# Plain values in rows of four tokens, spread by VectorE's 32x32 transposes, in an attention and FFN kernel

## The chip, the cores and the metric

The kernel runs on one core of a Trainium2 chip. The metric is the device time of one execution in microseconds (us), the median over runs. The program is one launch; inputs and output are float32 in HBM, and the kernel computes in bf16 with float32 accumulation.

## The reference, cut to what matters

```python
# q, k, v: (8 batches, 8 heads, 576 tokens, 64); w_in (512, 2048), w_out (2048, 512)
rel = pos[:, None] - pos[None, :]
plain   = (rel >= 0) & (rel < 32)                        # heads 0..3
dilated = (rel >= 0) & (rel < 128) & (rel % 4 == 0)      # heads 4..7
attn = softmax(where(mask, q @ k.T / 8, -1e9)) ; a = attn @ v
x = a.transpose(0, 2, 1, 3).reshape(4608, 512)
out = relu(x @ w_in) ** 2 @ w_out
```

Attention is local: a query of a plain head sees 32 tokens, one of a dilated head 32 tokens of its own residue modulo 4. The FFN behind it has most of the arithmetic.

## The kernel before, in words

Tokens are handled in FFN tiles: four of 256 tokens, then seven of 512. For each tile, `ffn_groups` gives a list of groups: first-layer groups (line 971: 128x128 weights, products into a PSUM tile `pf`, then ReLU on ScalarE at line 984 and the square on VectorE at line 987, into `h2T`), and second-layer groups (line 1027, from `h2T` and `w_out_sb`). A program written out by hand says what is done between the groups. The string `PROGRAM` is split at `|`; its first stretch runs before the first group, and one stretch after each group. The order in which the steps are recorded is the order of each engine's instructions, under a manual schedule; the tile framework adds a semaphore wait wherever it finds that an instruction touches memory that an earlier recorded one writes or reads.

Batch 0 is done in the head, by `first_step`. Heads go in pairs e = 0..3 (0 and 1 plain, 2 and 3 dilated); part 0 is tokens 0 to 255, part 1 the other 320. The letters are: `L` in front of a colon, a load; `T`, TensorE transposes of q and k (line 794); `C`, their copies out of PSUM (lines 801 to 812); `B`, the mask bias into a score tile (line 824); `S`, scores (line 846); `E`, exponential (line 854) and, for part 1, the mask product on VectorE (line 857); `P`, values times probabilities (line 884); `D`, row sums (line 900); `L` and `X` followed by digits, the reciprocal by logarithm and exponential on ScalarE (lines 907, 910); `M`, the product with it on VectorE into `xT` (line 917), the FFN's input. `s28x183`, `w` and `W` are products of zeros (line 764) that TensorE makes between. `u`, `m` and `g` are mask copies; `r`, `R` and `z` are the postponed ReLU and squares of the first two tiles of groups (ReLU of the second at line 990, on VectorE).

Values go into `vbd`: for a pair e and a block i of 64 tokens, a 128x128 tile with the pair's two heads on the diagonal and zeros beside them. It has two buffers, used by batch parity.

- Plain values of batch 0, part 0 (`plain`): four float32 loads from the SP queue (line 1066), 256 bytes for each token, then step `h`: two casting copies on VectorE (line 1140) into blocks 0 to 3.
- Plain values of batch 0, part 1: software loads from the POOL queue (line 197, codes `L0:v1s` and `L0:v1t`), straight into blocks 4 to 8 of `vbd` in bf16, 64 by 5 pieces of 128 bytes each. Batches 1 and 2 have their plain values loaded at the same line (`L1:v0dp`, `L1:v1dp`, `L2:vwp`).
- Dilated values: loaded into `vd`, and for part 1 spread by copies (line 247, steps `G`).
- Step `N` zeroes half of the dilated blocks (lines 1048 and 1049).

All of a stretch's loads and steps are recorded in its order, so the loads of the first stretch, which stand at its start, are recorded ahead of all of the head's steps. On the POOL queue the loads use eight semaphores in turn: the load number n waits, before it is issued, until the load number n - 8 has landed.

Of the kernel before, what the change touches and what calls it, by code (L numbers as in the profile page):

```python
# [12 lines left out]
RES = 4  # L13
# [22 lines left out]
def _masks(by_residue: bool = False) -> np.ndarray:  # L36

    j = np.arange(64)[:, None]
    c = np.arange(96)[None, :]
    tok = 4 * (c % 24) + c // 24
    near = ((tok - j >= 0) & (tok - j < WIN)).astype(np.float32)
    kr, km = j % RES, j // RES
    cc = np.arange(64)[None, :]
    rem = ((kr == cc // 16) & (cc % 16 - km >= 0)).astype(np.float32)
    c = np.arange(96)[None, :]  # L50
    far = ((c - j >= 0) & (c - j < WIN)).astype(np.float32)
    one = np.concatenate([near, rem, far], axis=1)
    p = np.arange(128)
# [6 lines left out]
    return np.concatenate([both, ident], axis=1).astype(ml_dtypes.bfloat16)  # L60
# [3 lines left out]
def kernel(  # L64
# [9 lines left out]
    nc = tc.nc  # L74
# [34 lines left out]
    h2_pool = ctx.enter_context(tc.tile_pool(name="h2", bufs=2))  # L109
# [11 lines left out]
    mk = const.tile([P, 256 + P], bf16, name="mk")  # L121
# [13 lines left out]
    xT = const.tile([P, KT, RING], bf16, name="xT")  # L135
    rb = [{nm: const.tile([(80, P, 80)[i], 2 * H * RES * D], bf16, name=f"{nm}b{i}") for nm in "qk"} for i in range(3)]
# [46 lines left out]

    def load_v(b: int, parts, which="pdr"):
# [6 lines left out]
        i0, i1 = 4 * p0, 4 if p1 == 1 else NB  # L191
        sides = [(hl, slice(64 * hl, 64 * hl + 64)) for hl in range(2)]
        for what in which:
            if what in "pst":
                for e in {"p": (0, 1), "s": (0,), "t": (1,)}[what]:
                    for hl, rows in sides:
                        nc.gpsimd.dma_start(  # L197
                            dst[rows, e, i0:i1, rows],
                            v[b, 2 * e + (hl ^ crossed(b, e)), 64 * i0 : 64 * i1, :].rearrange("(i p) d -> p i d", p=64),
                        )  # L200
            elif what == "d" and b == 1:
# [58 lines left out]

    def k_flat(e: int):

        return kbd[:, e, :, :].rearrange("p i c -> p (i c)")[:, 0:S]

    def trans_k(e: int):
# [12 lines left out]
        copy(k_flat(e).rearrange("p (m r) -> p m r", r=RES), x.rearrange("p r m -> p m r"))  # L278
# [95 lines left out]
    def quadrants(scs, pvs):  # L374
# [16 lines left out]
        for n, (b, e) in enumerate(pvs):  # L391
# [16 lines left out]
            for g, rows in enumerate(sides):  # L408
# [5 lines left out]
                def vrow(i):  # L414
                    return vbd[b % 2][rows, e, i, rows] if b == XB else v_rows[b % 2][rows, e, i, :]
# [108 lines left out]
    def batch1(code: str):  # L524
# [40 lines left out]
        elif what in "cp":  # L565
            nm, copy = code[1], nc.scalar.copy if code[3:] == "a" else nc.vector.tensor_copy
            x = two.pop((nm, int(what == "c")))
            if what == "c":
                copy(both_x[:, int(nm == "k"), H:, m0 : m0 + n], x)
            elif nm == "q":  # L570
                copy(qT[:, 0:2, :, m0 : m0 + n], x.rearrange("p (e r) m -> p e r m", r=RES))
            else:
                copy(
                    k_nat[:, :, RES * m0 : RES * m0 + w].rearrange("p e (m r) -> p e m r", r=RES),
                    x.rearrange("p (e r) m -> p e m r", r=RES),
                )
# [40 lines left out]
        elif what == "b":  # L617
# [6 lines left out]
            for e in (2, 3, 0, 1):  # L624
# [10 lines left out]
                for g, rows in enumerate(sides):  # L635
# [19 lines left out]
                    else:  # L655
                        y = 0
                        for i, _, q0, q1 in blocks(1, e, part):
                            z = RES * (q1 - q0)
                            to, rhs = slice(q0 - m0, q1 - m0), byr(two["n", e][rows, y : y + z])
                            P_.append((f"o{e}", o[cols, :, to], vbd[1][rows, e, i, rows], rhs, z))  # L660
# [107 lines left out]
    def first_step(code: str):  # L768
# [28 lines left out]
        elif what == "C":  # L797
# [9 lines left out]
            else:  # L807
                copy(qk0[:, 0, e, :, m0 : m0 + n], x[:, 0, :, :])
                nc.vector.tensor_copy(
                    xx[0][:, 1, S * e + RES * m0 : S * e + w + RES * m0].rearrange("p (m r) -> p m r", r=RES),  # L810
                    x[:, 1, :, :].rearrange("p r m -> p m r"),
                )
# [131 lines left out]
    def ffn_groups(tk0: int, nt: int):  # L944
# [4 lines left out]
        h2 = h2_pool.tile([P, NF, NT], bf16, name="h2T")  # L949
# [50 lines left out]
        def g1(i):  # L1000
# [5 lines left out]
            elif i < 4 and tk0 == 2 * NT:  # L1006
                for u, x in ((0, 0), (0, 1), (1, 0), (1, 1), (2, 0), (2, 1), (0, 2), (1, 2),
                             (2, 2), (3, 0), (3, 1), (3, 2), (0, 3), (1, 3), (2, 3), (3, 3))[4 * i : 4 * i + 4]:
                    mm1(u, kts[x : x + 1])
# [50 lines left out]
    plain = osb_pool.tile([P, DM], f32, name="osb")[:, :].rearrange("p (e i d) -> p e i d", e=2, d=D)  # L1060
# [3 lines left out]
    for e in range(2):  # L1064
        for hl, rows in enumerate(sides):
            nc.sync.dma_start(
                plain[rows, e, :, :], v[0, 2 * e + hl, 0:256, :].rearrange("(i p) d -> p i d", p=64)
            )
# [3 lines left out]
    near = mk[:, 0:96].rearrange("p (r m) -> p r m", r=RES)  # L1072

    def put(dst, src):
        nc.scalar.copy(dst, src)
# [4 lines left out]
    def masks(part):  # L1080
# [5 lines left out]
        if part:  # L1086
            put(r4(mask_p[:, 352:384]), near[:, :, 16:24])
            put(mask_p[:, 384:768].rearrange("p (i c) -> p i c", c=96), mk[:, 0:96].unsqueeze(1).broadcast_to([P, 4, 96]))
            put(r4(mask_p[:, 768:832]), near[:, :, 0:16])
            put(md[:, :, 0:32], mk[:, 224:256].unsqueeze(1).broadcast_to([P, RES, 32]))  # L1090
            put(md[:, :, 32:112], mk[:, 160:240].unsqueeze(1).broadcast_to([P, RES, 80]))
            put(mask_d[:, 704:768], mk[:, 96:160])
# [28 lines left out]
    def run(code):  # L1121
# [12 lines left out]
        elif code == "N":  # L1134
            zero_halves(vbd[0][:, NE // 2 :, 0:8, :])
        elif code[0] == "G":
            spread_v(0, int(code[1]), [int(code[2])], nc.scalar.copy if code[3:] else nc.vector.tensor_copy)
        elif code == "h":
            for rows in sides:
                nc.vector.tensor_copy(vbd[0][rows, 0:2, 0:4, rows], plain[rows, :, :, :])  # L1140
# [46 lines left out]
    for x, code in enumerate(("Q00", "Q01", "Q10", "Q11")):  # L1187
        steps.append((50 + x, 1, XB, code))
# [115 lines left out]
```

## Time and profile before

| | |
|---|---|
| time, median of 3 runs | 296.27 us (296.17 to 298.16) |
| the profiled execution: its time | 295.88 us |
| its span in the trace | 294.1 us |
| TensorE busy | 286.2 us, 97% |
| VectorE / ScalarE / GpSimd busy | 155.5 / 187.2 / 123.2 us |
| chain that ended last | TensorE 93% of the span |

A span is measured from the first to the last instruction of the trace; 1.8 us of the run lie around it. Times below are us from the start of the span. In a line of the timeline stand start, duration, engine, source line, operation, tile written and tiles read, shape, and count; the bracket at its end says how long the engine stood idle before it and what it waited for. A duration is that of the whole merged run of equal instructions; neighbours overlap by some hundredths of a us. PE is TensorE, DVE is VectorE, ACT is ScalarE, and POOL rows of DMA_DIRECT2D are the issues of software loads.

### The profile page before, as it was taken

The page shows a single profiled execution, that of the slowest core. Times are in us where ns is not written, and L with a number is a line of the kernel's source. Part 1 is how long each engine was busy: PE and PEld are TensorE (multiplying, and loading weights), DVE is VectorE, ACT ScalarE, POOL GpSimd, SP SyncE. Part 2 cuts the span into 40 slices and gives each one's busy share as a digit, 9 for nine tenths or more (in the row PEclk, how much of TensorE's full clock was granted, in tenths as well). Part 3 has the DMA queues.
Part 4 walks back from the last instruction along what each step waited for, and adds up shares of the span by engine and source line. Part 5 has one row for each costly group of instructions (what it writes and reads, how often), then busy time and mean ns, then how long its engine had stood idle before and what let it go on. Part 6 is the DMA issues. An engine that isn't in the chain of part 4 may idle for free.

```text
span 294.1 us, 7899 instructions
## 1 busy us (share of the span) xinstructions
PE 286.2 (97%) x3213; PEld 165.8 (56%) x3241; DVE 155.5 (53%) x452; ACT 187.2 (64%) x381; POOL 123.2 (42%) x208
## 2 busy tenths in 40 slices
PE   8999999999999999999999999999999999999994
PEld 6689647859555554555455545554554455445443
DVE  2785224647779566685659465947454245004300
ACT  6888545887667774988567656766676476127411
POOL 8686266847626965776763696000000000000000
PEclk9999999999999999999999999999999999999999
DMA  8999999999999999999999698012101210121022
GB/s 120 199 188 214 203 225 197 193 169 190 162 230 141 140 157 199 138 159 171 179 176 116 97 170 144 2 37 73 36 2 39 71 38 0 37 74 33 0 71 71
DMA packets 84211, 35.75 MB, mean 122 GB/s; under 512 B 53600, under 2 KB 79424, under 8 KB 84176
## 3 DMA queue, kind: packets, MB, share of 16 engines
q0 software_dynamic: 49056, 18.49, 56.5%
q1 hardware_dynamic: 34976, 16.67, 28.0%
q8 instruction: 25, 0.41, 0.6%
q10 hardware_dynamic: 144, 0.10, 0.1%
q14 instruction: 10, 0.08, 0.1%
HBM read 37.50 MB, written 9.44 MB: 160 GB/s over the span
## 4 chain that ended last, share of the span: by engine, by line
PE 93%; ACT 1%; issue 1%; DMA 1%; DVE 1%; POOL 0%; ACTq 0%; POOLq 0%
PE pf L1027 42%; PE pf L971 41%; PE po L369 2%; PE pa L369 2%; PE pf L369 1%; DMA kb<-in_k_dram 1%; ACT h2T L984 1%; PE pa L794 1%; PE pd L369 1%; PE pf L846 1%; DVE h2T L987 1%; PE po L764 1%; PE pa L564 0%; DVE qT L335 0%; PE po L884 0%
## 5 line engine op out<-in xcount | busy, mean ns | idle before, releaser
L971 PE MATMUL pf<-xT,w_in 128*128 128x512 bf16 (+1 forms) x697 | 127.6, 340 | 0.4
L1027 PE MATMUL pf<-w_out_sb,h2T 128*128 128x512 bf16 (+2 forms) x571 | 126.0, 373 | 1.6 <-issue 0.6
L984 ACT ACTIVATE h2T<-pf 128x512 bf16<-128x512 f32 x143 | 83.9, 600 | 32.3 <-PE pf L971 32.0
L971 PEld LDWEIGHTS <-w_in 128*128 128x128 bf16 x704 | 78.0, 113 | 46.3 <-issue 0.3
L987 DVE TENSOR_TENSOR h2T<-h2T 128x512 bf16<-128x512 bf16 x144 | 60.0, 424 | 61.5 <-ACT h2T L984 59.6
L1027 PEld LDWEIGHTS <-h2T 128*128 128x128 bf16 x592 | 56.1, 98 | 63.9
L321 POOL DMA_DIRECT2D vbd<-in_v_dram x80 | 43.5, 560 | 23.6 <-DMA kb<-in_k_dram 9.7
L1033 ACT COPY osb<-pf 128x512 f32<-128x512 f32 (+1 forms) x34 | 19.5, 574 | 50.5 <-PE pf L1027 50.5
L175 POOL DMA_DIRECT2D qb<-in_q_dram x19 | 13.7, 722 | 8.3 <-DMA xx<-qb 4.6
L713 ACT ACTIVATE rec<-rec 128x576 f32<-128x576 f32 x24 | 16.4, 683 | 0.7
L175 POOL DMA_DIRECT2D kb<-in_k_dram x19 | 13.3, 698 | 5.8 <-DMA w_in<-in_moe_w_in_dram 1.9
L197 POOL DMA_DIRECT2D vbd<-in_v_dram x16 | 11.0, 687 | 8.9 <-DMA kb<-in_k_dram 5.3
L730 ACT ACTIVATE pt<-pa 128x384 bf16<-128x384 f32 (+1 forms) x26 | 11.7, 498 | 4.5 <-DVE xT L720 3.8
L307 POOL DMA_DIRECT2D vd<-in_v_dram x20 | 12.0, 615 | 3.2 <-PE pa L369 2.1
L313 POOL DMA_DIRECT2D vbd<-in_v_dram x20 | 12.0, 618 | 3.2 <-PE pf L369 1.9
L716 DVE TENSOR_TENSOR xT<-pf,rec 128x512 bf16<-128x512 f32 x11 | 7.6, 692 | 10.5 <-ACT rec L713 10.5
L716 DVE TENSOR_TENSOR xT<-po,rec 128x512 bf16<-128x512 f32 x13 | 9.0, 691 | 6.5 <-ACT rec L713 6.3
L732 DVE TENSOR_TENSOR pt<-pt,mask_n 128x384 bf16<-128x384 bf16 (+1 forms) x20 | 7.2, 374 | 8.6 <-ACT pt L730 8.5
L732 DVE TENSOR_TENSOR pt<-pt,mask_f 128x384 bf16<-128x384 bf16 x24 | 8.4, 355 | 6.1 <-ACT pt L730 5.9
L369 PEld LDWEIGHTS <-vbd 64*64 64x64 bf16 x328 | 8.4, 107 | 4.4 <-issue 4.0
L337 DVE COPY qT<-xx 64x576 bf16<-64x576 bf16 (+1 forms) x30 | 10.5, 351 | 0.6
L730 ACT ACTIVATE pt<-pf 128x448 bf16<-128x448 f32 (+1 forms) x18 | 8.6, 519 | 1.0 <-PE pf L369 0.9
(156 smaller groups left out, 280.5 us busy)
## 6 DMA issues: line engine op xcount, KB each, us to landing
qb<-in_q_dram POOLq DMA_DIRECT2D x7, 320.0 KB, 6.8
kb<-in_k_dram POOLq DMA_DIRECT2D x7, 320.0 KB, 8.0
vd<-in_v_dram POOLq DMA_DIRECT2D x34, 64.0 KB, 4.5
w_out_sb<-in_moe_w_out_dram POOLq DMA_DIRECT2D x4, 512.0 KB, 13.0
out_dram<-osb SPq DMA_DIRECT2D x16, 128.0 KB, 5.0
qb<-in_q_dram POOLq DMA_DIRECT2D x6, 256.0 KB, 6.4
kb<-in_k_dram POOLq DMA_DIRECT2D x6, 256.0 KB, 8.8
out_dram<-osb SPq DMA_DIRECT2D x9, 160.0 KB, 3.7
```

The source lines that it names most:

```text
L175: nc.gpsimd.dma_start(t[p0 : p0 + n, part, h0:h1, :], src[b, h0:h1, t0 : t0 + RES * n, :].rearrange("h (p r) d -> p h (r d)", r=RES),)
L321: nc.gpsimd.dma_start(v_rows[b % 2][p0 + 16 * r : p0 + 16 * r + 16, e, :, :], v[b, 2 * e + hl, :, :].rearrange("(i m r) d -> r m i d", r=R ...
L369: nc.tensor.matmul(out, lhs, rhs, start=begin, stop=True, skip_group_check=True)
L713: nc.scalar.activation(rec[:, :], rec[:, :], ACT.Exp, scale=-1.0)
L716: nc.vector.tensor_tensor(out=tok[:, :, 16:M], in0=byr(o[:, :]), in1=byr(rec[:, 0:512]), op=ALU.mult)
L730: nc.scalar.activation(pt, sp[b, e][g][:, 0:n], ACT.Exp, scale=SCALE)
L732: nc.vector.tensor_tensor(out=pt, in0=pt, in1=mask, op=ALU.mult)
L971: nc.tensor.matmul(to, w_in_sb[piece][:, kt, c0 : c0 + 509 : 4], rhs, start=(kt == kts[0] and x == 0), stop=(kt == kts[-1] and x == per - ...
L984: nc.scalar.activation(hv, acc[u][:, :].rearrange("p (x n) -> p x n", x=per), ACT.Relu)
L987: nc.vector.tensor_tensor(out=hv, in0=hv, in1=hv, op=ALU.mult)
L1027: nc.tensor.matmul(cur[m][:, c0:c1], h2[:, f, P * m : P * m + P], w_out_sb[:, f, c0:c1], start=(f == 0), stop=(f == NF - 1),)
L1033: (nc.vector.tensor_copy if last and part == 1 or tk0 == 3 * NT // 2 else nc.scalar.copy)(osb[:, c0:c1], cur[m][:, c0:c1])
```

## The change

Plain values of batches 0 to 2 are loaded in rows of four tokens: partition 32f + x holds, for one head, the 256 values of the tokens 8x + 4f to 8x + 4f + 3 of a part. Such a load goes into the second halves of the `h2T` tiles, which the 256-token tiles do not use; `h2T` becomes two fixed tiles in place of a pool. A new step `A` (`place`) spreads a part: one VectorE 32x32 transpose over float32 words (two bf16 values each) within the staging tile, then further ones into `vbd`, two for batch 0 (one for each half of the partitions) and one for batches 1 and 2. The order of the tokens within a block that comes out is (f, m, r) for token 8m + 4f + r, so keys (`keys`) and masks are put into the same order: a key copy becomes two copies, and for part 1 or a whole sequence three.

The last 64 tokens (block 8) do not fit the pattern and get loads of their own, code `u`. The first part of batch 0 still comes from SP, as float32 in the new rows, with a casting copy `Z` into the staging tile. In the first stretch the steps `P00 P10 D00 D10 L00` move from behind `T31` to ahead of `S20`, three mask copies move from ScalarE to VectorE, `C31` from ScalarE to VectorE, `N` to the start, and most of the products of zeros go.

```diff
-    "L0:q001 L0:q023 L0:q123 L0:v0d L0:i0 L0:q101 L0:v1d L0:i1a L0:i1b L0:v1s L0:i2a L0:v1t L0:i2b L0:i3 L0:o0 L0:o1 "
-    "L0:o2 L0:o3 L1:q00123 y L1:q10123 L1:v0dp s28x183 T00 C00a T10 C10a B00 B10 w1 S00 E00 B20 W1 S10 E10 N u B30 W1 "
-    "w1 T20q w1 T20k C20v T30 C30v h W1 w1 S20 E20 w1 S30 E30 T21 C21v T31 C31a G20 G30 P00 P10 D00 D10 L00 X00 P20 "
-    "P30 D20 D30 L20 X20 M00 j S21 S31 w1+31 M20 E21 E31 G21 G31a | T01q T11q | T01k C01v T11k C11a r P21 P31 D21 D31 "
-    "R S01 S11 L21 X21 M21 L31 X31 M31 z E01 E11 | L2:q00123 L2:q10123 L1:v1dp |  | P01 D01 L01 X01 M01 P11 D11 L11 "
...
+    "L0:q001 L0:q023 L0:q123 L0:v0d L0:i0 L0:q101 L0:v1d L0:i1a L0:i1b L0:v1s L0:v1t L0:i2a L0:v1u L0:i2b L0:i3 L0:o0 "
+    "L0:o1 L0:o2 L0:o3 L1:q00123 y L1:q10123 L1:v0pd Z s40x128 T00 C00a T10 C10a B00 B10 S00 E00 B20 S10 E10 A00 u B30"
+    " T20q w1 T20k C20v T30 C30v P00 P10 D00 D10 L00 S20 E20 w1 S30 E30 T21 C21v T31 C31v X00 M00 P20 P30 D20 D30 L20 "
+    "X20 M20 G20 G30 S21 S31 w1+31 w1+31 j E21 E31 G21 G31a | T01q T11q | T01k C01v T11k C11a r P21 P31 D21 D31 R S01 "
+    "S11 L21 X21 M21 L31 X31 M31 A01 E01 E11 z | L2:q00123 L2:q10123 L1:v1pud |  | P01 D01 L01 X01 M01 P11 D11 L11 X11"
...
-    h2_pool = ctx.enter_context(tc.tile_pool(name="h2", bufs=2))
+    h2T = [const.tile([P, NF, NT], bf16, name=f"h2T{i}") for i in range(2)]
...
+    def fours(b: int, part: int):
+        x = 4 * (3 * (part == 0) if b == 0 else part + (b == 1))
+        t = h2T[b // XB]
+        return t[:, x : x + 2, NT // 2 :], t[:, x + 2 : x + 4, NT // 2 :]
+
+    def place(b: int, part: int):
+        x, y = (t.bitcast(f32) for t in fours(b, part))
+        nc.vector.transpose(y.rearrange("p e (x r) -> p e r x", r=RES), x.rearrange("p e (r x) -> p e r x", r=RES))
+        y = y.rearrange("p e (i x) -> p e i x", i=4)
+        at = slice(4 * part, 4 * part + 4)
+        for rows, cols in [(rows, rows) for rows in sides] if b == 0 else [(slice(0, P), slice(0, D))]:
+            nc.vector.transpose(vbd[b % 2][rows, 0 : NE // 2, at, cols].bitcast(f32), y[rows])
...
-                            dst[rows, e, i0:i1, rows],
-                            v[b, 2 * e + (hl ^ crossed(b, e)), 64 * i0 : 64 * i1, :].rearrange("(i p) d -> p i d", p=64),
+                            fours(b, part)[0][rows, e, :],
+                            v[b, 2 * e + (hl ^ crossed(b, e)), 256 * part : 256 * part + 256, :].rearrange("(x f r) d -> f x (r d)", f=2, r=RES),
...
+            elif what == "u":
+                for hl, rows in sides:
+                    nc.gpsimd.dma_start(
+                        dst[rows, 0 : NE // 2, NB - 1, rows if b == 0 else slice(0, D)],
+                        v[b, (slice(hl, H // 2 - hl, 3 - 2 * hl) if b else slice(hl, H // 2, 2)), 512:S, :].rearrange("h p d -> p h d"),
+                    )
...
+    def keys(copy, to, x, some: bool):
+        n = x.shape[2] - 16 * some
+        for f in range(2):
+            copy(
+                to[:, 0 : RES * n].rearrange("p (i f m r) -> p f i m r", f=2, m=8, r=RES)[:, f],
+                x[:, :, 0:n].rearrange("p r (i m f) -> p f i m r", m=8, f=2)[:, f],
+            )
+        if some:
+            copy(to[:, RES * n :].rearrange("p (m r) -> p m r", r=RES), x[:, :, n:].rearrange("p r m -> p m r"))
...
-        elif code == "h":
-            for rows in sides:
-                nc.vector.tensor_copy(vbd[0][rows, 0:2, 0:4, rows], plain[rows, :, :, :])
+        elif code == "Z":
+            nc.vector.tensor_copy(fours(0, 0)[0], plain[:, :].rearrange("p (e x) -> p e x", e=2))
+        elif code[0] == "A":
+            place(int(code[1]), int(code[2]))
```

The rest of the diff follows from this: later stretches of `PROGRAM` get `A10`, `A11`, `A20` and `A21` for batches 1 and 2, whose loads come as `L1:v0pd`, `L1:v1pud` and `L2:vwpu`; one q copy of batch 2 is made a group earlier, and two products of the fifth tile change places.

More of the change, by code (lines that the diff above doesn't have):

```diff
@@ L52, in _masks @@
     one = np.concatenate([near, rem, far], axis=1)
+    placed = near.reshape(8, 2, RES, 96).transpose(1, 0, 2, 3).reshape(64, 96)
     p = np.arange(128)
@@ L59, in _masks @@
         return np.concatenate([turned[:, 0:96]] * 4 + [close], axis=1).astype(ml_dtypes.bfloat16)
-    return np.concatenate([both, ident], axis=1).astype(ml_dtypes.bfloat16)
+    last = near.reshape(64, RES, 24)[:, :, 0:16].reshape(64, 64)
+    both = np.concatenate([np.concatenate([placed] * 2, axis=0), both[:, 96:], ident, np.concatenate([last] * 2, axis=0)], axis=1)
+    return both.astype(ml_dtypes.bfloat16)
 @with_exitstack
@@ L119 @@
     nc.scalar.preload_act_table_set("natural_log_exp_and_others")
-    mk = const.tile([P, 256 + P], bf16, name="mk")
+    mk = const.tile([P, 256 + P + 64], bf16, name="mk")
     ident = mk[:, 256 : 256 + P]
@@ L414, in vrow @@
                 def vrow(i):
[L415 removed]
+                    if b > XB:
+                        return v_rows[b % 2][rows, e, i, :]
+                    return vbd[b % 2][rows, e, i, rows if dil else slice(0, D)]
                 P_, D_ = [], []
@@ L572, in batch1 @@
             else:
[L573 to L576, printed above, removed]
+                for e in range(NE // 2):
+                    keys(copy, k_nat[:, e, RES * m0 : RES * m0 + w], x[:, RES * e : RES * e + RES, :], part)
         elif what == "s":
@@ L948, in ffn_groups @@
         early = NT <= tk0 <= 3 * NT
-        h2 = h2_pool.tile([P, NF, NT], bf16, name="h2T")
+        h2 = h2T[len(made) % 2]
+        made.append(tk0)
         per = NT // nt
@@ L1059 @@
             nc.scalar.copy(to, none)
-    plain = osb_pool.tile([P, DM], f32, name="osb")[:, :].rearrange("p (e i d) -> p e i d", e=2, d=D)
+    zero_halves(vbd[0][:, NE // 2 :, 0:8, :])
+    plain = osb_pool.tile([P, DM], f32, name="osb")
     nc.vector.tensor_scalar(
@@ L1063 @@
     )
-    for e in range(2):
-        for hl, rows in enumerate(sides):
+    for hl in range(2):
+        for f in range(2):
+            p0 = 64 * hl + 32 * f
             nc.sync.dma_start(
-                plain[rows, e, :, :], v[0, 2 * e + hl, 0:256, :].rearrange("(i p) d -> p i d", p=64)
+                plain[p0 : p0 + 32, :].rearrange("p (e x) -> p e x", e=2),
+                v[0, hl : H // 2 : 2, 0:256, :].rearrange("e (x f r) d -> f x e (r d)", f=2, r=RES)[f],
             )
```

27 lines of the change are left out of this document (11 added, 16 removed), and 12 rows, old and new, of the table PROGRAM.

## The prediction

> **What bounds the kernel now.** I read the page's first lines, then PE's waits, then PE's timeline, because the change works on the first 14 us alone and moves little behind them.
>
> ```profile
> span 294.1 us, 7899 instructions
> PE 286.2 (97%) x3213; PEld 165.8 (56%) x3241; DVE 155.5 (53%) x452; ACT 187.2 (64%) x381; POOL 123.2 (42%) x208
> ...
> PE po L764 <- DVE kbd L1051: 1.1, 1, 1.1
> ...
> PE pf L846 <- issue: 0.6, 1, 0.6
> PE pa L794 <- DMA kb<-in_k_dram: 0.3, 1, 0.3
> ```
>
> PE is the bound. The longest single waits of it are 1.1 us before the first instruction, 0.6 us in which nothing visible holds it, and 0.3 us for the first keys. All of them lie in the head. The timeline and the stretches show the rest:
>
> ```profile
> 9.06 0.29 PE L794 MATMUL pa<-mk,kb 64*64 64x64 bf16 x8
> ...
> 11.21 0.49 PE L884 MATMUL pf<-pt,vbd 128*128 128x96 bf16 x8
> 11.53 0.48 PE L900 MATMUL pf<-pt,ones 128*128 128x96 bf16 x8
> ...
> 14.38 1.04 PE L971 MATMUL pf<-xT,w_in 128*128 128x256 bf16 x8
> ...
> 18.84 2.81 PE L971 MATMUL pf<-xT,w_in 128*128 128x256 bf16 x24
> ...
> 1.07:4.42 3.35, 3.35 (x23) 3.30 (x24) 0.47 (x4) 3.31 (x4) 3.15 (x5) 1.00 0.71 117
> 4.42:4.98 0.56, 0.56 (x8) 0.42 (x5) 0.00 (x0) 0.53 (x2) 0.56 (x2) 1.00 1.42 205
> 5.00:14.38 9.38, 8.46 (x214) 5.77 (x214) 6.05 (x18) 6.78 (x18) 6.98 (x12) 1.00 1.33 188
> 14.38:18.84 4.46, 4.46 (x97) 3.76 (x96) 3.65 (x10) 3.39 (x9) 4.16 (x6) 1.00 1.41 194
> ```
>
> From the first FFN product (14.38) on PE is busy without a gap, so the time is the start of the FFN plus a fixed amount of PE work: what delays the head is not won back behind it, and what shortens the head is won in full. The head has 9.38 - 8.46 = 0.9 us of idle PE between 5.00 and 14.38.
>
> **The plain values: a new wait.** Before, the plain values of part 0 need SP's loads and two casting copies. The software loads of part 1 (L197) go to other blocks of the same tile, and the copies pass them:
>
> ```profile
> 9.81 0.86 DVE L1140 CAST vbd<-osb 64x512 bf16<-64x512 f32 x2
> ...
> 12.12 0.72 POOL L197 DMA_DIRECT2D vbd<-in_v_dram  x1
> 14.26 0.67 POOL L197 DMA_DIRECT2D vbd<-in_v_dram  x1 [1.42 <-DMA w_in<-in_moe_w_in_dram]
> ...
> 15.92 1.36 POOL L197 DMA_DIRECT2D vbd<-in_v_dram  x2
> 17.27 1.52 POOL L1105 DMA_DIRECT2D w_in<-in_moe_w_in_dram  x2
> ...
> L197 POOL DMA_DIRECT2D vbd<-in_v_dram x4: 674/686/722, 12.1 to 16.6; - x4
> ...
> DMA to landing us min/median/max: 4.7/5.1/5.3
> ```
>
> The copies run at 9.81, before any of those four loads is issued. In the changed program as built this is otherwise. The two transposes of A00 that write into `vbd` each wait for two DMA semaphores, at the value that the 21st and the 22nd software load bring them to. These are the two loads of `L0:v1u`, for the last 64 tokens. They stand ahead of A00 in the program, and write block 8 of the same tile; the transposes write blocks 0 to 3 through a float32 view of it. No byte is shared, but the wait is there. P00 on PE waits for the second of those transposes.
>
> So the question is when `u` lands. Load n is issued when load n - 8 has landed. Loads 16 to 22 were v1s, v1s, i2a, v1t, v1t, i2b, i3 (the POOL rows above, i2a's left out; the second of the last pair at about 18.0), and are v1s, v1s, v1t, v1t, i2a, u, u; what each waits for, loads 8 to 14, is unchanged. So `u` is issued at 17.3 and 18.0. The bytes queued ahead of it and with it are those of the old v1s, i2a and v1t, whose last was issued at 16.6 and landed 4.7 later, at 21.3. I take 21.3 for the second `u`: the queue was full then, and it holds as much now.
>
> ```profile
> L313 POOL DMA_DIRECT2D vbd<-in_v_dram x20: 586/611/657, 69.8 to 172.0; - x20
> ...
> DMA to landing us min/median/max: 2.3/4.5/7.4
> ```
>
> Line 313 issues loads of values into the same tile too. Bounds: its shortest landing gives 18.0 + 2.3 = 20.3, the longest of L197 18.0 + 5.3 = 23.3.
>
> The Trainium skill ("DMA: Bandwidth & Descriptors", section "Why a DMA increments its semaphore by 16 and not by 1") has a DMA run on the largest number of engines up to 16 that divides the slowest dimensions of both sides. The new four-token loads have 2 there, which would queue each on two engines and could bring `u` up to an estimated 1 us later; no run here shows it yet, and the upper bound holds it already.
>
> **What stands behind the wait.** VectorE works in order: behind A00 stand three mask copies (moved from ScalarE), C20, C30, C21, C31, M00. PE does its work up to T30 and stops at P00, which now stands ahead of S20. PE made T30's keys at 9.06 before, and with fewer zeros does so a little sooner. So it stands for about 12 us. Ahead of P00 the change thus gains nothing: the fewer zeros, `Z`, `A00`'s first transpose and the doubled part-0 key copies all end long before 21.3 and cost nothing under that cover.
>
> From 21.3 the chain is made of these rows:
>
> ```profile
> 9.14 0.76 DVE L801 COPY xx<-pa 128x512 bf16<-128x512 bf16 x2 [0.90 <-PE pa L794]
> 11.03 0.49 DVE L801 COPY xx<-pa 128x640 bf16<-128x640 bf16 x1 [0.36 <-PE pa L794]
> 11.44 0.21 DVE L803 COPY kbd<-pa 128x64 bf16<-128x64 bf16 x1
> 12.30 1.06 DVE L247 COPY vbd<-vd 64x256 bf16<-64x256 bf16 x4
> 13.39 0.69 DVE L917 TENSOR_TENSOR xT<-pf,rec 128x512 bf16<-128x512 f32 x1
> 14.00 0.46 DVE L1143 CAST vbd<-osb 64x128 bf16<-64x128 f32 x2
> ...
> 15.10 0.79 DVE L857 TENSOR_TENSOR pt<-pt,mask_d 128x512 bf16<-128x512 bf16 x2
> ...
> 17.13 0.33 DVE L808 COPY xx<-pa 128x320 bf16<-128x320 bf16 x1 [0.49 <-PE pa L794]
> 17.37 0.88 DVE L809 COPY xx<-pa 128x320 bf16<-128x320 bf16 x2
> 18.17 0.68 DVE L990 TENSOR_SCALAR h2T<-pf 128x512 bf16<-128x512 f32 x1
> ...
> 8.96 0.80 ACT L1075 COPY mask_d<-mk 128x128 bf16<-128x128 bf16 x3
> ...
> 12.05 0.60 ACT L907 ACTIVATE rec<-pf 128x512 f32<-128x512 f32 x1
> 12.68 0.63 ACT L910 ACTIVATE rec<-rec 128x512 f32<-128x512 f32 x1
> ```
>
> - The second spread transpose, 64 partitions by 512 bf16: no row has a transpose. Nearest is a copy of that size (0.86 / 2 = 0.43, from float32; a bf16 copy of half the size takes 0.26). I take 0.35; bounds 0.2 to 0.7. It ends at 21.65.
> - Mask copies: 0.80 for three on ScalarE; on VectorE I take 0.2 each, as the smallest copies there (0.21): 22.25.
> - C20, C30: 0.76, to 23.0. Meanwhile PE does P00, P10, D00, D10 (0.49 + 0.48 by the rows), then S20, S30 and T21, T31, to about 23.9.
> - C21 and now C31 as well on VectorE, 2 x (0.49 + 0.21) = 1.4, to 25.0; before, ScalarE took C31's large half.
> - M00 0.69, to 25.7. L00 and X00 (0.60 + 0.63 behind D00) are done by then. The first FFN product comes at 25.7 instead of 14.38: **+11.3**.
> - Then VectorE sets the pace up to the third FFN stretch: M20 behind X20, to 26.6 (I allow 0.2 of waiting); G20, G30 1.06; j 0.46; mask products of E21, E31 0.79; G21's two copies 0.5: 29.4. Then the key and query copies C01, C11 (0.33 + 0.88, and 0.3 more because each key copy is now three): 30.9; the postponed ReLU 0.68: 31.6. PE alone would be there at 25.7 + 4.46 = 30.2. Before, the third stretch began at 18.84, as that ReLU ended (18.17 + 0.68). So **+12.75**: the part of VectorE's head work that used to run during the head's PE work now stands behind the stall.
>
> Behind it A01 (three transposes, 1.1 by the value above) comes ahead of P01 and E01's mask product; PE has its 2.8 us of FFN meanwhile, and v1s and v1t have landed by 21.3, so I cost it at nothing. Without that cover it is at most its 1.1.
>
> **PE's clock.** PE's 183-column products show a cold start: 3.35 us hold 23 (146 ns each), the next 0.56 us hold 8 (70 ns each). A stop of 12 us may bring the slow state back. P00 to T31 hold about 1.8 us of PE work and the stretch behind some 4.5, of which VectorE hides much; I take +0.5, bounds 0 and 1.2.
>
> The Trainium skill ("TensorE: Matmul & The Clock Gate", section "Part 1: The HAM clock gate (the "warmup" mystery)") has the clock fall after some 3.4 us of idle and need as long of busy time to return. By it the upper half of those bounds would hold; the cold start agrees (146 against 70 ns), while no stop long enough to test the fall is in the trace.
>
> **The sum.** 294.1 + 12.75 + 0.5 = 307.35 us of span. The profiled execution took 295.88, 1.78 more than its span, so 309.1; the median (296.27) lies 0.4 above that execution: **309.5 us**. Bounds: landing -1.0 and +2.0, transpose -0.15 and +0.35, clock -0.5 and +0.7, VectorE's pieces about 0.7 either way. Added up in full they give 307.2 to 313.2, the likeliest case's own range.
>
> **Rival 1: no stall, not slower.** The place is A00, the deciding point whether `u` is in by about 9.5, when P00 could begin. Then P00, D00 and L00 run ahead of S20 and M00 comes earlier. The head's idle PE time bounds the gain: 1.1 us, which stays (it lies before the first instruction), and 0.9 us. I give it 0 to 0.6: 295.7 to 296.3. Against it: POOL issues the 22nd load at 18.0, and nothing ahead of it is taken out; the chip would have to pass a wait that stands in the program. A gain of over 1% (3 us) exceeds all idle time of the head, so it hardly exists.
>
> **Rival 2: the change doesn't do what it says.** The plain products come first, but the first FFN tile also needs M20, and X20 ahead of it now stands behind four more products of about 1 us (0.49 + 0.48 for the rows of two pairs). If M20 is what the first tile really waits for, the new order brings nothing even without a stall, and the time is the old 296.3. For it: the reciprocals run one behind the other on ScalarE, 0.60 + 0.63 us each by the rows above. With the stall it is a detail inside the 12.75.
>
> **Rival 3: a second stall.** A10 waits in the same way for `L1:v1u`.
>
> ```profile
> 43.88 0.70 DVE L616 TENSOR_TENSOR pt<-pt,mask_p 128x352 bf16<-128x352 bf16 x2
> ...
> 46.67 0.76 POOL L197 DMA_DIRECT2D vbd<-in_v_dram  x1
> 48.00 0.67 POOL L197 DMA_DIRECT2D vbd<-in_v_dram  x1 [0.58 <-DMA kb<-in_k_dram]
> ...
> DMA to landing us min/median/max: 4.4/6.6/10.0
> ```
>
> A10 stands behind that mask product, at 44.6, and with the shift at about 57.8. By its place in the queue `L1:v1u` has the slots of 46.67 and 48.00; the landings of 36 to 60 us (last row) put it at 52.4 to 58.0. So it is in by then, but narrowly. If the loads slip 1 to 3 us, PE loses up to 3 us again: 310.5 to 312.5.
>
> **How the numbers follow.** Forecast (one stall, 307.2 to 313.2) 0.84; second stall 0.08, within the same range; no stall or nothing done (rivals 1 and 2) 0.06; over 1% faster 0.02. About 1%, 3 us, is what a measurement of this kernel can tell from no change. Slower is the first two cases, 0.92; of the third 0.05 are the same and 0.01 a gain larger than I can name, which with the last makes faster 0.03. The range reaches down to 304.5, for a `u` that lands sooner than its bound and VectorE work that the stall hides after all, and up to 313.5.
>
> **What would show it.** Right: VectorE idle from about 9 to 21 before a transpose into `vbd`, ended by a DMA of values; PE idle about 12 us before line 884's first product; first FFN product at 24.5 to 28; third stretch 12 to 14 us later than 18.84; from there on the old timeline, shifted. The clock: the products behind the stall at double their old time for the first few us. Rival 3: a second idle of VectorE of that kind near 58. Wrong: no idle on VectorE over 2 us in the head, or `u` landing before 15; then the time is near 296 and the reading of the wait was mistaken. If the stall is there and the time is below 304, the PE work behind it was not fixed.

## The result: slower by 6.0%, more than forecast, and the profile after

The changed kernel takes 314.62 us (median of 6 runs, 312.22 to 315.76) against 296.26 us before: 1.0603 times, 95% interval 1.0557 to 1.0648. That is 18.4 us more; 13.2 were forecast, and the time lies 1.1 us above the range. The stall that was forecast is there, at its place and nearly with its length. What was mis-sized is the work behind it: PE's at a lower clock, VectorE's, and that of the later steps `A`. Every ratio here counts only runs within 1.5% of the fastest of their kernel, while a median counts all; of u_behind_zeros below it counts 303.01 and 305.29 us.

The first lines of the page of after (the slices of PEclk are 7.8 us each, 9 is full speed):

```profile
span 313.3 us, 7979 instructions
PE 291.0 (93%) x3220; PEld 169.0 (54%) x3248; DVE 162.9 (52%) x485; ACT 185.8 (59%) x379; POOL 129.1 (41%) x218
PEclk9555999999999999999999999999999999999999
```

Its waits, of VectorE:

```profile
DVE vbd L203 <- DMA vbd<-in_v_dram: 13.3, 1, 13.3
```

and of PE (total, times, longest):

```profile
PE pf L921 <- DVE vbd L203: 12.3, 1, 12.3
PE po L804 <- DVE kbd L1089: 1.1, 1, 1.1
PE pa L409 <- DVE kbd L388: 0.9, 1, 0.9
PE po L921 <- DVE pt L894: 0.6, 1, 0.6
```

VectorE stood 13.3 us at A00's transposes into `vbd` until a load of values landed, and PE 12.3 us behind it. PE's busy time also rose, by 4.8 us, although it does less: some of it ran at half speed. VectorE's timeline of after, with the two rows of A00 and the first copy of C21:

```profile
7.87 0.63 DVE L199 STREAM_TRANSPOSE h2T<-h2T 128x256 f32<-128x256 f32 x1
21.84 0.91 DVE L203 STREAM_TRANSPOSE vbd<-h2T 64x256 f32<-64x256 f32 x2 [13.35 <-DMA vbd<-in_v_dram]
...
26.12 0.49 DVE L841 COPY xx<-pa 128x640 bf16<-128x640 bf16 x1 [2.03 <-PE pa L834]
```

And PE's, from T30's keys to the fifth FFN stretch:

```profile
10.11 0.40 PE L834 MATMUL pa<-mk,kb 64*64 64x64 bf16 x8
22.81 0.77 PE L921 MATMUL pf<-pt,vbd 128*128 128x96 bf16 x8 [12.30 <-DVE vbd L203]
23.39 0.78 PE L937 MATMUL pf<-pt,ones 128*128 128x96 bf16 x8
...
29.69 1.92 PE L1009 MATMUL pf<-xT,w_in 128*128 128x256 bf16 x8
...
35.36 2.89 PE L1009 MATMUL pf<-xT,w_in 128*128 128x256 bf16 x24
38.88 0.39 PE L921 MATMUL po<-pt,vbd 128*128 128x32 bf16 x6 [0.64 <-DVE pt L894]
...
39.78 9.77 PE L1009 MATMUL pf<-xT,w_in 128*128 128x256 bf16 x88
```

The first FFN product came at 29.69 (before 14.38), the third stretch at 35.36 (before 18.84). The products behind the stall take 0.77 and 0.78 us where they took 0.49 and 0.48, and the first eight FFN products 1.92 where they took 1.04. The stretches of the timeline say why. After the colon stand the length, then busy time of PE, PEld, DVE, ACT and POOL, and behind them PE's granted clock, the DMA share and GB/s:

```profile
5.00:8.00 3.00, 1.93 (x50) 1.28 (x47) 1.36 (x6) 0.65 (x3) 3.00 (x6) 1.00 1.38 189
8.00:10.50 2.50, 2.50 (x43) 1.46 (x42) 0.49 (x1) 1.70 (x5) 1.65 (x4) 0.55 1.38 193
10.50:22.80 12.30, 0.01 (x2) 0.00 (x0) 0.89 (x3) 0.00 (x0) 9.74 (x16) 0.50 1.22 161
22.80:32.10 9.30, 9.29 (x145) 6.64 (x145) 5.93 (x18) 4.78 (x10) 4.91 (x7) 0.50 1.08 196
32.10:35.40 3.30, 3.30 (x79) 2.75 (x76) 2.85 (x12) 1.65 (x4) 0.73 (x1) 0.99 1.07 216
```

The granted clock was 0.50 through the stall and for 9.3 us of unbroken PE work behind it.

### The profile page after: what moved, and what is told of

Its sections match the earlier page's. It is cut to its first block, busy times and chain, and to the rows that moved or that the text cites. A ratio compares the mean times of both kernels' runs of the same rounds, so it can differ in the third digit from the quotient of the medians.

```text
span 313.3 us, 7979 instructions
## 1 busy us (share of the span) xinstructions
PE 291.0 (93%) x3220; PEld 169.0 (54%) x3248; DVE 162.9 (52%) x485; ACT 185.8 (59%) x379; POOL 129.1 (41%) x218
## 4 chain that ended last, share of the span: by engine, by line
PE 79%; DMA 11%; DVE 5%; POOL 2%; issue 1%; ACT 1%; SPq 0%; DVEq 0%; ACTq 0%; POOLq 0%
PE pf L1065 35%; PE pf L1009 35%; DMA xx<-qb 7%; DMA w_in<-in_moe_w_in_dram 2%; DVE h2T L1025 2%; PE po L409 2%; DMA vbd<-in_v_dram 1%; PE pa L409 1%; PE pf L409 1%; PE pa L834 1%; PE pd L409 1%; POOL qb L179 1%; POOL h2T L217 1%; PE pf L883 1%; POOL kb L179 1%
## 5 line engine op out<-in xcount | busy, mean ns | idle before, releaser
L361 POOL DMA_DIRECT2D vbd<-in_v_dram x80 | 43.6, 560 | 27.2 <-DMA kb<-in_k_dram 12.5
L217 POOL DMA_DIRECT2D h2T<-in_v_dram x20 | 13.3, 671 | 10.0 <-DMA w_out_sb<-in_moe_w_out_dram 3.6
L353 POOL DMA_DIRECT2D vbd<-in_v_dram x20 | 11.9, 613 | 5.1 <-PE pf L409 2.1
L921 PE MATMUL pf<-pt,vbd 128*128 128x96 bf16 (+3 forms) x17 | 1.2, 226 | 12.3 <-DVE vbd L203 12.3
```

Source lines behind the costliest of these rows:

```text
L217: nc.gpsimd.dma_start(fours(b, part)[0][rows, e, :], v[b, 2 * e + (hl ^ crossed(b, e)), 256 * part : 256 * part + 256, :].rearrange("(x f ...
L361: nc.gpsimd.dma_start(v_rows[b % 2][p0 + 16 * r : p0 + 16 * r + 16, e, :, :], v[b, 2 * e + hl, :, :].rearrange("(i m r) d -> r m i d", r=R ...
```

## The experiments

Each kernel is compared with the kernel before on its own chip. "Shift" below is how much later ScalarE's ReLU of the same FFN group ran than in the profile of before; a time given with a shift is the group's time there.

### Is the wait for `u` the stall, and is there nothing else?

**u_behind_both**: the loads `u` recorded behind the steps that waited for them.

```diff
- ... L0:v1t L0:i2a L0:v1u L0:i2b ... L1:v0pd Z ... E10 A00 u B30
+ ... L0:v1t L0:i2a Z ... E10 A00 L0:v1u L0:i2b ... L1:v0pd u B30
- L2:q10123 L1:v1pud | ... | 1s1 A11 |
+ L2:q10123 L1:v1pd | ... | 1s1 A11 L1:v1u |
```

> The changed kernel with the loads of the last 64 tokens recorded behind the transposes that were made to wait for them: in the first stretch L0:v1u and the loads that follow it stand behind A00 (the order on the POOL queue stays), and L1:v1u stands behind A11. Theory (the wait for u is the whole stall, and the rest of the loss is PE's half clock, which fell at about 8.3 us, ahead of the stall): the 12.3 us of idle PE go, the first FFN product comes at 15 to 18, but PE still runs part of the head at a granted clock of 0.5; time 297 to 301. Rival 1 (the clock fell only because of the stall, and the change is otherwise what it promises): 295 to 296.5. Rival 2 (the stall is the wait for the values themselves or for another load, not for u): 312 to 316 again.

Measured: 308.62 us, 1.0349 times before (1.0282 to 1.0416). The early stall is gone, and the clock still fell; but the time fits no expectation: it lies between the theory's and rival 2's. The shift was 4.1 us at 26 us and 13.2 from 89 us on. Where the other 9 came from stands in that kernel's waits of PE, in VectorE's timeline and in the stretches:

```profile
PE pf L1055 <- DVE h2T L189: 3.9, 1, 3.9
```

VectorE's timeline, A11 and the second transpose of A20:

```profile
59.50 0.66 DVE L189 STREAM_TRANSPOSE h2T<-h2T 128x256 f32<-128x256 f32 x1 [2.07 <-DMA h2T<-in_v_dram]
...
86.50 0.45 DVE L193 STREAM_TRANSPOSE vbd<-h2T 128x256 f32<-128x256 f32 x1 [4.96 <-DMA vbd<-in_v_dram]
```

The stretches of low clock (columns as above):

```profile
8.00:18.90 10.90, 10.90 (x187) 7.62 (x183) 6.49 (x21) 6.22 (x15) 7.69 (x13) 0.53 1.31 184
...
90.00:96.50 6.50, 5.92 (x79) 2.99 (x80) 2.86 (x8) 2.68 (x6) 4.66 (x9) 0.50 1.27 203
```

A11 (at 59.50) waits 2.07 us for its values and A20 (at 86.50) 4.96 us for the loads `u` of batch 2. PE, starved for 3.9 us by the latter, then runs 6.5 us at a clock of 0.50. In the changed kernel these steps began 11 and 12 us later (A11 at 70.46; A20's first transpose at 92.48, here at 80.91) and did not wait: the early stall had covered later ones.

**u_behind_A00**: the first stretch altered in the same way, `L1:v1pud` left in its place.

> As the one before, but only the first stretch is altered: L1:v1u stays ahead of A10. Theory: with the head no longer late, A10 is due near 46 to 49 us and waits for L1:v1u, which landed at 56.4 in the changed kernel and would land at 52 to 57; VectorE stands for 4 to 9 us and PE, fed by it, loses 2 to 8 us: time 300 to 307, and above the kernel without either wait. Rival (PE has enough work in hand, or the load is in by then): the same as the kernel without either wait, within 1 us.

Measured: 309.04 us, 1.0376 (1.0317 to 1.0436). The second stall of the prediction's rival 3 appeared, at its place, once the first one was out of the way. VectorE's timeline, PE's waits, and the stretches around it:

```profile
58.03 0.45 DVE L193 STREAM_TRANSPOSE vbd<-h2T 128x256 f32<-128x256 f32 x1 [7.09 <-DMA vbd<-in_v_dram]
```

PE's wait for it:

```profile
PE po L399 <- DVE vbd L193: 6.0, 1, 6.0
```

The stretches:

```profile
52.60:54.90 2.30, 0.00 (x0) 0.00 (x0) 0.00 (x0) 1.26 (x3) 0.48 (x1) 0.97 1.41 203
54.90:58.50 3.60, 0.00 (x0) 0.00 (x0) 0.47 (x2) 0.00 (x0) 2.93 (x6) 0.50 1.00 114
58.50:61.70 3.20, 3.17 (x39) 1.53 (x40) 2.82 (x11) 1.29 (x3) 3.20 (x6) 0.52 0.97 102
```

A10 waited 7.09 us, PE 6.0. Yet the total is that of the kernel without this wait (expected: above it, and 300 to 307). The delay of 6 us at A10 spared A11 and A20 theirs (none of VectorE's waits for a load belongs to them): one stall took the place of the others.

**pairs_apart**: the order of the changed kernel, with the writes to `vbd` cut by pairs.

```diff
-            nc.vector.transpose(vbd[b % 2][rows, 0 : NE // 2, at, cols].bitcast(f32), y[rows])
+            for e in range(NE // 2):
+                nc.vector.transpose(vbd[b % 2][rows, e, at, cols].bitcast(f32), y[rows, e])
-                        dst[rows, 0 : NE // 2, NB - 1, rows if b == 0 else slice(0, D)],
+                        dst[rows, e, NB - 1, rows if b == 0 else slice(0, D)],
```

> The changed kernel in its own order, but each transpose into vbd and each load u is cut in two, one for each pair e (two more transposes per step of batch 0, one more for the others; four loads u for a batch instead of two). Theory (the wait is no need of the data: a write to both pairs at once spans, from its first to its last address, the other's block 8, and cut by pairs the spans lie apart): no step A waits for a load u, the stall of 12.3 us goes as it did with u behind the steps, the clock still falls near 8 us; 304 to 310. Rival (the wait has another ground, such as the float32 view itself): 312 to 317.

Measured: 304.15 us, 1.0227 (1.0167 to 1.0287), in the expected range: no step A stalls for `u` (A10 and A11 wait 1.08 and 2.32 us for their values). The clock fell only at 13.94 in its profile, not near 8 us as expected, and came back at 17.35. A00's transposes in VectorE's timeline:

```profile
8.10 1.01 DVE L204 STREAM_TRANSPOSE vbd<-h2T 64x128 f32<-64x128 f32 x4
```

P00 and P10 in PE's:

```profile
9.23 0.49 PE L923 MATMUL pf<-pt,vbd 128*128 128x96 bf16 x8
```

So the wait was no need of the data, and no matter of the float32 view alone: it went when the stretches of memory from first to last address lay apart. That such stretches overlap is not enough for a wait either. In the kernel before, step `h` writes blocks 0 to 3 of both pairs at once, as bf16, and the loads `L0:v1s`, recorded ahead of it, write blocks 4 to 8 of pair 0, between its first and its last address; yet `h` ran at 9.81, before the first of them was issued at 12.12. Which of the differences makes the wait (the float32 view of the write, the load across both pairs) is not shown: this run cut the write and the load together. With the wait for `u` gone in either way the loss falls from 6.0% to 2.3 to 3.5%. The stall costs 7.5 to 11 us net (the difference of the ratios times 296 us), less than its 12.3.

### What did the zeros do?

**u_behind_zeros**: the kernel of u_behind_both with the zeros of before (`s28x183`, and `w1`, `W1` as in the old string up to P00).

> The kernel without either wait, and the products of zeros in the first stretch as they were before the change (28 of 183 columns at the start, then nine of 256 or 512 columns up to P00 instead of one). Theory (the clock falls near 8 us because the head's PE work has gaps since the zeros went): the granted clock stays at 1.00 through the head; time 295.5 to 297.5, and 1 to 4 us below the kernel with few zeros. Rival (the zeros only take PE time): 0.5 to 1.5 us above the kernel with few zeros, their own column time.

Measured: 306.69 us in the median (303.01 to 308.51), 1.0212 (1.0114 to 1.0309). The clock was 1.00 through the head, and ScalarE's first ReLU came 0.5 us later than before instead of 3.3. The total missed its range for the reason found above: between 54 and 69 us the shift grew from 3.3 to 9.6, and there stand a clock of 0.50 from 63.65 to 70.48 us of the run's own time and, ahead of it, A11's wait, in VectorE's timeline:

```profile
59.80 0.64 DVE L189 STREAM_TRANSPOSE h2T<-h2T 128x256 f32<-128x256 f32 x1 [3.34 <-DMA h2T<-in_v_dram]
```

**before_few_zeros**: the kernel before, with the few zeros.

```diff
- ... s28x183 T00 C00a T10 C10a B00 B10 w1 S00 E00 B20 W1 S10 E10 N u B30 W1 w1 T20q ... h W1 w1 S20 ...
+ ... s40x128 T00 C00a T10 C10a B00 B10 S00 E00 B20 S10 E10 N u B30 T20q ... h S20 ...
```

> The kernel before, with only the products of zeros of the first stretch thinned out as in the changed kernel (40 of 128 columns at the start instead of 28 of 183; one of 512 columns up to S20 instead of nine). Theory (without them PE has gaps in the head, the granted clock falls to 0.5 near 8 us and stays there until full-size products have run for some 3 us): first FFN product at 15.5 to 18 instead of 14.4, time 2 to 5 us above before. Rival (the zeros only take PE's time): 0 to 1 us below before, clock 1.00 throughout.

Measured: 296.54 us, 0.9983 (0.9942 to 1.0024): no difference. The clock did fall, but only from 11.09 to 14.50 us, and the first FFN product came at 15.20, 0.8 us later than before. The theory was right that it falls, and wrong on when it comes back (ahead of the first FFN product) and on its price, and the fewer zeros are no part of the 18 us by themselves.

### What is the half clock worth behind the stall?

**stall_filled**: zeros for the stall.

```diff
- ... T30 C30v P00 P10 ...
+ ... T30 C30v w45 P00 P10 ...
```

> The changed kernel with 45 products of zeros (512 columns each) on PE between T30 and P00, so that PE works while VectorE waits for u; nothing else differs, and the wait for u is kept. Theory (of the 18.4 us lost, 12.3 are the stall and 4 are the half clock behind it): the clock is back at 1.00 when P00 starts at about 22 to 23, the first FFN product comes at 25.5 to 27.5 instead of 29.7, the third stretch at 31.5 to 33.5 instead of 35.4; time 310 to 312.5. Rival (VectorE's chain sets the pace behind the stall, the slow products hide under it): the third stretch stays at 34.5 to 35.5 and the time at 313.5 to 315.

Measured: 316.94 us, 1.0642 (1.0570 to 1.0713): no gain, the theory's time is refuted. But P00 and the first FFN product, in PE's timeline, came where it says, and the third stretch (34.13) between its range and the rival's:

```profile
11.12 11.46 PE L794 MATMUL po<-kbd 128*128 128x512 bf16 x45
22.99 0.49 PE L911 MATMUL pf<-pt,vbd 128*128 128x96 bf16 x8 [0.41 <-DVE vbd L193]
...
27.27 1.04 PE L999 MATMUL pf<-xT,w_in 128*128 128x256 bf16 x8
...
34.13 2.86 PE L999 MATMUL pf<-xT,w_in 128*128 128x256 bf16 x24
...
94.87 0.23 PE L399 MATMUL pa<-qT,kbd 64*64 64x96 bf16 x2 [1.92 <-issue]
```

The first FFN product came 2.4 us sooner, the third stretch only 1.2: PE stood 1.56 us at 31.68 for a mask product that VectorE had behind step `j`, whose two casts took 1.98 us there and 0.48 in the changed kernel. Behind that PE lost the rest again, in waits like the 1.92 us of the last row for which the profile shows no cause but its own sequencer. To measure the clock alone, the later steps A had to go.

**after_again**, the changed kernel on the chip of the next three:

> The changed kernel once more, on the chip of the three runs beside it, so that they can be compared with it: 313 to 317, PE idle for 12 us ahead of P00, granted clock 0.50 from about 8 to about 32 us.

Measured: 314.05 us, 1.0611 (1.0556 to 1.0666). Here the clock fell only at 13.19 us, in the stall itself, and came back at 30.26: what it was before the stall did not change the time.

**stall_b0**: early stall and few zeros as in the change, batches 1 and 2 loaded as before, without A10 to A21.

```diff
- ... L1:v0pd ... L1:v1pud ... A10 ... A11 ... L2:vwpu ... A20 | | A21 ...
+ ... L1:v0dp ... L1:v1dp ... L2:vwp ...
```

> The changed kernel with its early stall and its few zeros, but with the plain values of batches 1 and 2 loaded as before and without A10, A11, A20, A21 (keys and masks keep the new order, so the output of these two batches is not the reference's). Theory (the 1.8 us that the changed kernel loses between 54 and 117 us come from those steps and their loads): the shift against before stays near 17.3 us from 40 us to the end; time 1 to 2.5 us below the changed kernel. Rival (they come from the split key copies or from DMA traffic that all versions have): the shift grows to 19 all the same.

Measured: 314.54 us, 1.0605 (1.0576 to 1.0634), not below the changed kernel. In its profile the `u` loads were issued 1.5 us later, and P00 ran at 23.91 instead of 22.86; why is not shown. Counted from there, the theory holds: the shift was 18.17 us at 26 us and 18.50 at the end, a growth of 0.3; in the two profiles of the changed kernel it grew by 1.8 and 1.6.

**stall_b0_filled**: the same with `w45`.

> As the one before, with 45 products of zeros between T30 and P00. It measures the price of the half clock behind the stall where no later wait covers it. Theory (12.55 us from P00 to the third FFN stretch with the half clock, 11.14 without it, since VectorE is the next bound): 1 to 2 us below the kernel without the filling, third stretch near 34. Rival 1 (PE's whole slow stretch counts): 3.5 to 4.5 us below. Rival 2 (something gives it back later): no difference.

Measured: 314.58 us, 1.0596 (1.0557 to 1.0635): rival 2. The stretch from P00 to the third FFN stretch without the filling (stall_b0):

```profile
23.90:36.20 12.30, 12.29 (x218) 9.13 (x218) 8.65 (x29) 6.39 (x14) 5.99 (x9) 0.65 1.07 200
```

and with it:

```profile
23.70:34.20 10.50, 8.94 (x217) 7.04 (x217) 8.69 (x30) 6.35 (x14) 4.75 (x7) 1.00 1.10 206
```

and a later row of PE's timeline with the filling:

```profile
77.15 0.35 PE L406 MATMUL pf<-pt,ones 64*64 64x96 bf16 x16 [2.10 <-issue]
```

For the same work PE was busy 12.29 us at a mean clock of 0.65 and 8.94 us at 1.00. P00 came at 23.91 and the third stretch at 36.20 in the one, at 23.78 and 34.21 in the other: 12.29 against 10.43 us. So the half clock costs 1.9 us there, and VectorE's pace hides 1.5 of the 3.35. Then 2.10 us are lost at once at 77.15 in a wait named "issue". Both filled kernels have one of some 2 us, the unfilled ones with the stall none over 0.2; why it comes stays open.

### What is left without any stall?

**batch0_only**: no waits for `u`, zeros of before, batches 1 and 2 loaded as before.

> The changed kernel without the waits for u, with the zeros of before, and with the plain values of batches 1 and 2 loaded as before (straight into vbd, in their own order of tokens, while keys and masks keep the new order: the output of these two batches is therefore not the reference's). A10, A11, A20, A21 are gone. Theory (the 9 us that were lost behind 26 us without the early stall came from the steps A of batches 1 and 2, which wait for loads that PE itself would have needed only later): the shift against before stays at 2 to 4 us from 26 us to the end; time 2 to 5 us above before. Rival (the loss lies in the key copies or in DMA contention): 7 to 10 us above before.

Measured: 299.14 us, 1.0082 (1.0038 to 1.0127). The shift is 2.3 us at 26 us and 2.4 at the end: the theory holds, the 6 us that u_behind_zeros lost behind 26 us were those of A10 to A21 and their loads, and by the same steps' waits so are the 9 of u_behind_both.

**order_only**: the kernel before with the new order of steps alone.

```diff
- ... S20 E20 w1 S30 E30 T21 C21v T31 C31a G20 G30 P00 P10 D00 D10 L00 X00 P20 P30 D20 D30 L20 X20 M00 j S21 S31 w1+31 M20 E21 ...
+ ... P00 P10 D00 D10 L00 S20 E20 w1 S30 E30 T21 C21v T31 C31a X00 M00 P20 P30 D20 D30 L20 X20 M20 G20 G30 S21 S31 w1+31 j E21 ...
```

> The kernel before, with only the order of the first stretch changed as in the changed kernel: P00 P10 D00 D10 L00 ahead of S20, and M00, M20, G20, G30 in their new places; zeros, values, keys and masks as before. Theory (the head had 0.9 us of idle PE, nothing else to win): within 1 us of before either way, first FFN product between 13.9 and 15. Rival (M20 decides and comes later by the moved products): 1 to 2 us above before.

Measured: 299.62 us, 1.0080 (1.0053 to 1.0107), 2.4 us above before: beyond both ranges (the interval, 1.6 to 3.2 us, reaches into the rival's), and for another reason. VectorE's timeline, copies of the values (step `h`) and G21:

```profile
10.40 0.86 DVE L1130 CAST vbd<-osb 64x512 bf16<-64x512 f32 x2
...
19.30 0.79 DVE L237 COPY vbd<-vd 64x256 bf16<-64x256 bf16 x2
```

PE's, P00 and P21:

```profile
11.32 0.49 PE L874 MATMUL pf<-pt,vbd 128*128 128x96 bf16 x8 [0.95 <-DVE vbd L1130]
...
20.14 0.54 PE L874 MATMUL po<-pt,vbd 128*128 128x80 bf16 x8 [0.85 <-DVE vbd L237]
```

P00, moved ahead, stands 0.95 us for VectorE's copies of the values, and P21 0.85 us for the spreading copies that now come behind M20. In this profile, 4.5 us longer than before's, the clock was also at 0.50 from 20.26 to 23.68, so the two waits are not all of it.

**batch0_old_order**: batch0_only with the order of before in the first stretch.

> The kernel of batch0_only (no waits for u, zeros of before, batches 1 and 2 loaded as before, their output not the reference's) with the steps from S20 to the end of the first stretch in the order of before. Theory (what was left of the loss there, 0.8%, is the order plain products first, which alone cost 0.8%): within 0.4% of before. Rival (it is the work of the new values and keys themselves on VectorE): 0.6 to 1.2% above before.

Measured: 298.68 us, 1.0062 (1.0040 to 1.0083): the rival, at the lower edge of its range. Most of what remains there (1.8 of the 2.8 us of shift at the end) comes at one wait, `PE po L918 <- DVE pt L891: 1.6`: E01's mask product, which P01 needs, stands on VectorE behind A01's three transposes, and A01 waited 0.75 us for `u`.

No version was faster than the kernel before.

## Why the prediction was right and wrong

- **Right: the wait.** The stall was foreseen from the waits in the program and the landing times: 21.84 measured against 21.3 for its end, 12.3 us of idle PE against 12, and pairs_apart and u_behind_both show that it is the wait for `u`. The 1 us that the prediction allows for the spread of the four-token loads over engines has no working, and no run isolates it; these loads landed 4.6 to 7.3 us after their issue in the head, the old ones 4.7 to 5.3. Rival 1 (no stall) fell. Rival 2 was right in so far as the new order wins nothing by itself: order_only is 2.4 us above before. The wait of rival 3 is shown by u_behind_A00: PE's 6.0 us, hidden in the changed kernel by the first stall.
- **Wrong: how far PE's head work lies beside VectorE's ("PE's clock", +0.5, bounds 0 and 1.2).** It costs 1.9 us in the pair stall_b0 and stall_b0_filled, and in the changed kernel 2.1: from P00 to the third stretch 12.55 us, against 10.43 in stall_b0_filled with the clock at 1.00 (11.14 in stall_filled, with its long step `j`). The step that failed is "of which VectorE hides much". The clock stayed at 0.50 for 9.3 us of PE work; in the pair this work grew by 3.35 us, and VectorE's hid only 1.5 of them. C21 began at 26.12, where the sum has 23.6 (25.0 less its 1.4), 1.2 of it for the later P00: VectorE stood 2.03 us for T21 (the row at 26.12; 1.05 in stall_b0_filled), and so it did not set the pace.
- **Wrong: the transposes into `vbd`.** I set one behind the wait, 0.35 us, though I had read that each of the two waits for `u`. They took 0.91 in all: both stand behind it. With the landing (0.5 late), P00 came at 22.81 instead of 21.65, +1.2.
- **Mis-sized: VectorE's pieces** up to the third stretch: 10.43 us against 9.95 by the prediction's sum, inside its bounds of 0.7. The sum lacks one cost, which stands in all five profiles with the early stall: each copy or cast that VectorE began while one of POOL's two MEMSETs ran ended 0.08 us behind the end of a MEMSET, and took up to 1.06 us where such a copy takes 0.21 to 0.23 otherwise. (Before, the MEMSETs ran at 26.04, beside products of two tensors, which took their usual 0.42 to 0.43.) In the changed kernel these are the rows, of POOL and of VectorE:

```profile
28.62 0.94 POOL L1166 MEMSET qb<- 16x1024 bf16 x1
29.51 0.94 POOL L1166 MEMSET kb<- 16x1024 bf16 x1
...
29.66 1.82 DVE L273 COPY vbd<-vd 64x256 bf16<-64x256 bf16 x4
```

The four copies took 1.06 before. No run moves the MEMSETs: that they hold the copies up is read from the times alone.
- **Wrong: A01 "at nothing".** PE waits 0.64 us for E01's mask product behind it (row at 38.88); the shift grows by 0.8 there. Its bound of 1.1 was named, but not put into the range.
- **Wrong: nothing lost further on ("from there on the old timeline, shifted").** The shift grows from 17.3 to 19.1 between 54 and 117 us; with A10 to A21 taken out by 0.3 only.

Together: 1.2 + 0.5 + 2.1 - 0.5 + 0.8 + 1.8 = 5.9, and the span was 313.3 instead of 307.35. The 2.1 and the first 0.5 share one measured stretch, the 12.55 us, and are split by another kernel's 10.43.

## What to carry to other kernels

A wait that a program puts between accesses that share no byte can be read from the built instructions before the run; a load into one corner of a tile and a strided write across it are the place to look, and here cutting both so that the address spans lie apart took it away. A stall is costed with what follows it: TensorE's work behind this one ran at half clock for 9.3 us, of which 1.9 us remained beside VectorE's work. And a stall hides the stalls behind it: taking it away shows the next, so that the gain is less than its length.

## What the runs showed of the hardware

The records of the granted clock change on a grid. In every trace here the stretches between two changes are whole multiples of 3.41 us (a trace's last one apart): in the changed kernel the clock was full from 4.83 to 8.24 us, one such step, and half to 32.14, seven; in after_again it was half from 13.19 to 30.26, five; in before_few_zeros from 11.09 to 14.50, one. So how long after the start of some work the clock comes back depends on where that work lies on the grid. In stall_filled it came back at 14.34 us, 3.2 us after full-size products of zeros began. The stretches of that kernel:

```profile
11.12:14.40 3.28, 3.28 (x12) 1.19 (x9) 0.00 (x0) 0.00 (x0) 1.36 (x3) 0.51 1.35 199
14.40:22.90 8.50, 8.18 (x38) 3.53 (x36) 0.85 (x2) 0.00 (x0) 7.66 (x13) 1.00 1.18 150
```

It came back at 61.59 in u_behind_A00, 3.1 us after PE restarted mostly on FFN work. The Trainium skill ("TensorE: Matmul & The Clock Gate", section "Part 1: The HAM clock gate (the "warmup" mystery)") gives some 3.4 us of sustained work, in a window that runs freely and not from the kernel's start; the traces agree on its length and on that.

A step in which PE is busy throughout is not always enough. These are such a step of the changed kernel, one of before_few_zeros, and the stretch behind the latter:

```profile
25.31:28.72 3.41, 3.41 (x90) 2.82 (x86) 1.75 (x5) 1.83 (x4) 1.22 (x3) 0.50 1.15 215
...
11.09:14.50 3.41, 3.41 (x72) 2.73 (x68) 1.88 (x8) 2.23 (x5) 2.24 (x4) 0.50 1.33 195
14.51:15.20 0.69, 0.69 (x32) 0.54 (x26) 0.68 (x2) 0.66 (x2) 0.56 (x2) 1.00 1.38 192
```

After the first the clock stayed at 0.50, after the second it was back at 1.00, though neither holds an FFN product. The first holds all 32 of its head's last transposes of q and k, the second some 14; no run tests whether that is the difference. Nor does the fall need a full stop: in the changed kernel the clock fell at 8.24 us, behind a step (4.83 to 8.24) in which PE was busy for 2.34 of 3.41 us, and in u_behind_A00 at 54.76, 2.2 us after PE stopped at 52.5. Where a trace has no record of the clock yet, its views say 1.00: in the profile of before that is so up to 4.41 us, while the products took 146 ns each.

A VectorE 32x32 transpose of 128x256 float32 took 0.63 us within `h2T`, one of 64x256 into `vbd` 0.44 to 0.46, and half as large 0.25.
